# Pooled attention with an expert layer: the next pair's bounds ahead of the unit, and its K and V loads a step earlier

## The chip, the cores and the metric

The kernel runs on one core of one Trainium2 chip. The metric is the device time of the whole program in microseconds; the median of three runs before the change is 814.76 us (811.82 to 815.16). The profiled execution took 813.32 us.

## The reference

Attention over 4 batches and 8 heads with 64 columns; Q is averaged over pairs of neighbouring rows, so 576 rows of Q meet 1152 rows of K and V. Behind it, per row of 512 columns, a norm and two dense layers with a residual:

```
q_pool = q.reshape(B, H, S // 2, 2, D).mean(axis=3)
scores = q_pool @ k.transpose(0, 1, 3, 2) / sqrt(D)
attn   = softmax(scores) ; x = attn @ v            # then heads side by side: (4, 576, 512)
xn     = (x - mean) / sqrt(var + 1e-6) * g_ln
out    = x + maximum(xn @ w_ch1, 0) @ w_ch2
```

All is fp32. The kernel multiplies in fp16 with a high and a low half of each operand. So that the halves keep their precision it first looks for the largest absolute value of each Q, K and V (a bound), and scales by the power of two that this gives.

## The kernel before

**Tiling.** The heads go in pairs: 16 pairs, four to a batch (numbered from 0; p below). A pair has 576 x 2 rows of scores, worked in 9 steps of 128 rows, so there are 144 steps (i), and some 20 more in which only the dense layers run. The pair's first step is 9p; `i0 = (p - 1) * C` (L824) is the first step of the pair before it, and it is in those nine steps that pair p is prepared. The first batch (steps 0 to 35, `on_pe`) transposes its probabilities on TensorE. All later steps split them into a high and a low half and let a DMA transpose them (L440).

**One step** (`step`, L987) writes instructions in a fixed order, and each engine runs its own in that order. The minimum of the negated scores of step i on VectorE (`emit_max`, L410); the scores of step i + 1 on TensorE (`emit_s`, L390 and L398); then `flush`, which writes all that is kept in the list `evacs` (what empties the PSUM banks of the step before, on ScalarE and VectorE); the exponential and the high half on ScalarE (L417, L428); the low half of step i - 1 on VectorE, or on GpSimd in three of nine steps (L435 to L438), and the DMA transpose of that step on SP's queue; the output of step i - 4 on TensorE (`a_piece`, L480); one unit of the dense layers (`some_units`: 24 matmuls of L631, or 12 of L663); one preparation of pair p (`a_prep`); last what `todo` holds for the step, loads among it.

**PSUM.** Scores take two slots of three banks. In the third bank of a slot lie, side by side, the last 128 columns of the scores, the output (`ps` in L461) and the small results of the bounds (L193). The minimum of the next step reads that bank, so it waits for all that TensorE was told before to write there. ScalarE takes the scaled output from there (L540), and the scores two steps on wait for that. Units and preparations use banks 6 and 7 (`bank`, L552): if both are taken, `release` (L603) first writes what empties one.

**The bounds of pair p.** ScalarE takes the absolute maximum of each partition of K, Q and V (`bound`, L182) at steps i0 - 2 (Q), i0 + 1 (K) and i0 + 2 (V). At step i0 + 3 (step 3 of nine) `all_max` starts: TensorE transposes the maxima (L197), VectorE reduces them and sets up a diagonal (L200, L201). At step i0 + 4 TensorE spreads the result over all partitions (L208, "the spread"), and VectorE makes the scales of it (L231 to L234). K, Q and V are split with these.

**The preparations** (`PREPS`, L356) transpose K and Q on TensorE, one in each step from i0 + 4 on; ScalarE makes the high and VectorE the low half (L274, L271). GpSimd splits V in two halves (`take_v`, L239 and L266) at steps i0 + 5 and i0 + 7. K (`kr`) and V (`vr`) have one buffer each, so K of the next pair can't land before the last K preparation, nor V before V's second split. SP's queue carries the loads of K (two issues, L117 and L118), V (L121) and Q (L129), the stores (L684) and the transposes (L440), in the order in which they are written.

Of the kernel before, what the change touches and what calls it, by code (L numbers as in the profile page):

```python
# [24 lines left out]
def tile_pooled_attention_moe(  # L25
# [18 lines left out]
    nc = tc.nc  # L44
# [4 lines left out]
    C = S // 128  # L49
    HP = H // 2  # L50
# [109 lines left out]
    def pool_q(p, eng):  # L160
        x = raws[p, "q"]
        eng.tensor_tensor(x[:, :, 0], x[:, :, 0], x[:, :, 1], op=ALU.add)

    def dup_q(p, eng):
        x = raws[p, "q"]
        eng.tensor_copy(x[:, :, 1], x[:, :, 0])
# [171 lines left out]
    def prep_q_first():  # L338
# [17 lines left out]
    PREPS = (  # L356
        ((prep_k, 0), (prep_k, 2), (prep_q, 0), (prep_q, 1), (prep_k, 1), (prep_q, 2)),
        ((prep_k, 0), (prep_k, 2), (prep_q, 0), (prep_k, 1), (prep_q, 2), (prep_q, 1)),
    )


# [2 lines left out]
    def on_pe(i):  # L364

        return 0 <= i < HP * C
# [38 lines left out]
    def emit_max(i):  # L405

        st = steps[i]
        st["pe"] = p_p.tile([128, S], FP32, tag="pe", name="pe", bufs=3)
        nb = st["nb"] = sm_p.tile([128, 1], FP32, tag="nb", name="nb")
        nc.vector.tensor_tensor_reduce(  # L410
            out=st["pe"], in0=st["s"], in1=nought[:, 0:1].to_broadcast([128, S]),
            scale=pair[i // C]["sc"][:, 0:1], scalar=3.0e38, op0=ALU.add, op1=ALU.min, accum_out=nb,
        )

    def emit_exp(i):
        st = steps[i]
        nc.scalar.activation(out=st["pe"], in_=st["pe"], func=ACTF.Exp, scale=-1.0, bias=st["nb"])  # L417
# [32 lines left out]
    def emit_t_copy(i):  # L450
        st = steps[i]
        for a, b in ((0, 512), (512, S)):
            nc.scalar.copy(st["pt"][:, a:b], st["s"][:, a:b])  # L453
# [98 lines left out]
    def bank():  # L552
        for _ in range(2):
            for _ in free_banks:
                nbank[0] += 1
                n = nbank[1] = free_banks[nbank[0] % len(free_banks)]
                if n not in held and n not in waiting:
                    waiting.add(n)
                    return psum[:, n]
            n = nbank[0] + 1  # L560
            while free_banks[n % len(free_banks)] in held:
                n += 1
            release(free_banks[n % len(free_banks)])
# [34 lines left out]
    evacs, last = [], []  # L598

    def until(fns, n=None):  # L600
        evacs.extend((n, fn) for fn in fns)

    def release(n):  # L603
        waiting.discard(n)
        while any(m == n for m, _ in evacs):
            evacs.pop(0)[1]()

# [204 lines left out]
    def at(i, fn, *a):  # L812
        todo.setdefault(i, []).append((fn, a))
# [3 lines left out]
    def pre(i, fn, *a):  # L817
        early.setdefault(i, []).append((fn, a))
# [3 lines left out]

    for p in range(1, NP):
        i0 = (p - 1) * C  # L824
        at(max(i0 - 1, 0), load, p, "k", nc.sync)
        at(i0, load, p, "v", nc.sync)
        at(i0 + 1, bound, p, "k")
        if p == 1:
            pre(0, behind_scales)
            pre(i0 + 1, pool_q, p, nc.gpsimd)  # L830
            at(i0 + 1, dup_q, p, nc.gpsimd)
            at(i0 + 2, bound, p, "q")
        elif on_pe(i0):
            at(i0 - 4, load_q, p, (nc.sync,))
            at(i0 - 1, lambda p=p: calm.appendleft((lambda n: pool_q(p, nc.gpsimd), 0)))
            at(i0, lambda p=p: calm.appendleft((lambda n: dup_q(p, nc.gpsimd), 0)))
            at(i0 + 2, bound, p, "q")
        else:
            early_q = not on_pe(i0 - 6)
            at(i0 - (12 if early_q else 8), load_q, p, (nc.sync,))  # L840
            at(i0 - (6 if early_q else 4), pool_q, p, nc.vector)
            at(i0 - 2, bound, p, "q")
            at(i0 - 1, dup_q, p, nc.gpsimd)
        if not on_pe(p * C):
            at(i0 + 2, bound, p, "v")
        pre(i0 + 3, scales_reduce, p, 0, 2 if on_pe(p * C) else 3)
        for n in range(2):
            if on_pe(p * C):
                at(i0 + (5, 7)[n], gate)
            at(i0 + (5, 7)[n], take_v, p, n)  # L850
        for n, (fn, u) in enumerate(PREPS[p % HP // 2]):
            late = 1 if on_pe(i0) else 0
            pre(i0 + 4 + n + late, lambda fn=fn, p=p, u=u: preps.append((fn, p, u)))

# [24 lines left out]
    norms, fresh, turns = deque(), deque(), set()  # L879
# [79 lines left out]
    def a_prep():  # L959
        if preps:  # L960
            fn, p, u = preps.popleft()
            until(fn(p, u), nbank[1])
# [6 lines left out]
    def a_piece(i):  # L969
        pieces.extend(ready.pop(i, ()))  # L970
        for u in range(2 if len(pieces) > 2 and not on_pe(i) else 1):
            if pieces:
                n = pieces.popleft()
                pt = pts[n]
                ps = emit_pv(n, bank() if u or on_pe(n) else None)
                if on_pe(n):
                    ot = pt.rearrange("p a n -> p (a n)").bitcast(FP32)[0:65, 0:128]
                    until([lambda ot=ot, ps=ps: nc.scalar.activation(
                        out=ot, in_=ps[0:65, 0:128], func=ACTF.Identity, bias=eps
                    )], nbank[1])  # L980
                    turned.append((n, ot))
                    continue
                one, two = evac_pv(n, ps)
                until([one], nbank[1] if u else None)
                last.extend((two, lambda n=n: evacuated(n)))

    def step(i):  # L987
        live = i < NSTEP
        this[0] = i
        for fn, a in early.pop(i, ()):  # L990
            fn(*a)
        if live:
            emit_max(i)
        if on_pe(i - 1):
            emit_t_copy(i - 1)
            steps.pop(i - 1)
        while found:
            found.popleft()()
        first = on_pe(i - 1) or on_pe(i)
        final, last[:] = list(last), []  # L1000
        if first and not on_pe(i):
            a_piece(i)
        if on_pe(i):
            if i < 3:
                warm(16, bank())
            a_piece(i)
            a_prep()
            emit_exp(i)
        while scaled_out:
            scaled_out.popleft()()  # L1010
        if i + 1 < NSTEP:
            emit_s(i + 1)
            pv_slot[0] = i + 1
        else:
            free_banks[:] = [6, 7, 0, 1, 3, 4]
            pv_slot[0] += 1
        if on_pe(i):
            while fill:
                drip()
            flush()  # L1020
        else:
            flush()
            if live:
                emit_exp(i)
                emit_hi(i)
        for fn in final:
            fn()
        if 0 <= i - 1 < NSTEP and not on_pe(i - 1):
            emit_lo(i - 1)
            steps.pop(i - 1)  # L1030
            drip()
        norm(i)
        norms.extend(fresh)
        fresh.clear()
        red = None
        while soon or len(fill) > 3:
            drip()
        if on_pe(i):
            emit_t(i)
            if reds:  # L1040
                found.append(reds.popleft()())
        elif reds:
            red = reds.popleft()
            put = [None]

            behind = i % C == 3 or i % C == 4 and i not in turns
            if not behind:
                until([lambda: put[0]()])
        while turned:
            n, ot = turned.popleft()  # L1050
            emit_turn(n, ot, i)
        if not on_pe(i):
            if not first:
                a_piece(i)
            if red and not behind:
                put[0] = red()
            if i in turns:
                a_prep()
            some_units(i)
            if red and behind:  # L1060
                until([red()])
            if i not in turns:
                a_prep()
        for fn, a in todo.pop(i, ()):
            fn(*a)
        if calm and i < HP * C - 1:
            gate()
        for _ in range(1 if i < HP * C - 1 else 2):
            if calm:
                fn, n = calm.popleft()  # L1070
                fn(n)

    def warm(n, ps=None):
        ps = psum[:, 2, 0:128] if ps is None else ps[:, 0:128]
        for _ in range(n):
            nc.tensor.matmul(out=ps, lhsT=ident16, rhs=ident16, start=True, stop=True)

    with tc.manual_schedule():
# [67 lines left out]
        i = 0  # L1146
# [32 lines left out]
```

## Time and profile before

| | |
|---|---|
| median of three runs | 814.76 us |
| profiled execution | 813.32 us, span 811.5 us |
| TensorE busy | 781.8 us (96%) |
| VectorE, ScalarE, GpSimd busy | 598.6 (74%), 544.0 (67%), 342.5 us (42%) |
| granted TensorE clock | 1.00 of full speed in the whole span |
| DMA in 157 to 700 us / 700 to 811.5 us | busy share 0.86 / 0.06 |

The first batch ends near 157 us; from there to some 700 us attention and the dense layers share the steps (4.4 to 5.5 us each); behind that only dense layers are left. In the rows further down PE is TensorE, PEld its weight loads, DVE VectorE, ACT ScalarE, POOL GpSimd and SPq the DMA queue of SyncE. What stands in brackets behind an instruction is how long its engine stood idle before it, and which engine's instruction ended that.

### The profile page before, as it was taken

Reading aid. Unit: us, or ns where it says so; the run is one execution under the profiler, and the core shown is the slowest. Engines: PE = TensorE matmul, PEld = TensorE weight load, DVE = VectorE, ACT = ScalarE, POOL = GpSimd, SP = SyncE. Lnnn points to the kernel's source line nnn. Section 1 sums busy time; section 2 is a strip of 40 time slices with the busy share of each in tenths; the row PEclk is TensorE's granted clock in tenths of the full one; section 3 lists DMA queues with packets and bytes.
Section 4 is the critical chain, followed back from the end, with each engine's and each line's share of the span. In section 5 each row is a group of like instructions: output and inputs, shape, how many; then the busy total and the mean of one; then the engine's idle time right before and its main releaser. Section 6 shows DMA issues by size and latency. Waiting matters only on the chain.

```text
span 811.5 us, 21278 instructions
## 1 busy us (share of the span) xinstructions
PE 781.8 (96%) x8936; PEld 551.8 (68%) x8936; DVE 598.6 (74%) x1179; ACT 544.0 (67%) x789; POOL 342.5 (42%) x342
## 2 busy tenths in 40 slices
PE   8999999989989999989999999999999999999997
PEld 6788887767565656567666665767575757766764
DVE  5899999878898986898687877887786867521221
ACT  5889888777767777787677686877677776211010
POOL 2012333576999862665453535537161532300000
PEclk9999999999999999999999999999999999999999
DMA  9736545025998989896989798987979786401001
GB/s 282 241 107 219 192 135 172 2 72 109 168 181 154 179 167 201 164 213 116 202 143 220 147 212 145 186 163 144 197 135 196 131 145 121 86 1 27 14 1 27
DMA packets 276017, 115.95 MB, mean 143 GB/s; under 512 B 259280, under 2 KB 259280, under 8 KB 275920
## 3 DMA queue, kind: packets, MB, share of 16 engines
q1 hardware_dynamic: 275440, 113.63, 67.9%
q8 instruction: 70, 1.15, 0.6%
q10 hardware_dynamic: 480, 0.95, 0.4%
q14 instruction: 27, 0.22, 0.1%
HBM read 46.14 MB, written 4.72 MB: 63 GB/s over the span
## 4 chain that ended last, share of the span: by engine, by line
PE 63%; DVE 16%; ACT 7%; DMA 6%; issue 4%; SPq 2%; POOL 2%; ACTq 0%; DVEq 0%
PE psum L663 19%; PE psum L631 17%; PE psum L390 7%; PE psum L480 6%; PE psum L471 5%; DVE pe L410 5%; PE psum L447 3%; DVE hl L437 3%; DMA vr<-in_v_dram 2%; PE psum L398 2%; ACT pe L417 2%; SPq L440 2%; DMA kr<-in_k_dram 1%; DMA stage<-in_moe_w_ch_dram 1%; PE psum L321 1%
## 5 line engine op out<-in xcount | busy, mean ns | idle before, releaser
L410 DVE CUSTOM_DVE_ANT_0 pe<-psum,nought,sc 128x1152 f32<-128x1152 f32 x144 | 203.0, 1410 | 25.2 <-PE psum L197 9.7
L417 ACT ACTIVATE pe<-pe,nb 128x1152 f32<-128x1152 f32 x144 | 180.4, 1253 | 32.4 <-DVE nb L410 31.2
L663 PE MATMUL psum<-wsl,ht 128*128 128x512 f16 x864 | 196.6, 379 | 2.5 <-DVE ht L645 2.1
L631 PEld LDWEIGHTS <-wsl 128*128 128x128 f16 x1920 | 169.6, 98 | 25.3 <-issue 7.6
L631 PE MATMUL psum<-xn,wsl 128*128 128x256 f16 x1536 | 176.3, 273 | 6.6 <-DVE xb L677 3.8
L663 PEld LDWEIGHTS <-ht 128*128 128x128 f16 x864 | 81.1, 98 | 90.9 <-issue 3.1
L428 ACT ACTIVATE hl<-pe 128x1152 f16<-128x1152 f32 x108 | 125.6, 1163 | 3.4
L390 PE MATMUL psum<-kt,qt 64*128 64x512 f16 (+1 forms) x960 | 120.2, 380 | 1.0 <-ACT qt L274 0.7
L644 ACT ACTIVATE ht<-psum 128x512 f16<-128x512 f32 x72 | 42.7, 593 | 115.4 <-PE psum L631 112.2
L437 DVE SCALAR_TENSOR_TENSOR hl<-pe,hl 128x1152 f16<-128x1152 f32 x72 | 113.3, 1573 | 0.0
L480 PE MATMUL psum<-vt,pt 128*128 128x65 f16 (+2 forms) x3240 | 106.8, 193 | 0.0
L645 DVE SCALAR_TENSOR_TENSOR ht<-psum,ht 128x512 f16<-128x512 f32 x72 | 49.3, 685 | 72.3 <-ACT ht L644 72.3
L480 PEld LDWEIGHTS <-pt 128*128 128x128 f16 (+1 forms) x3240 | 98.4, 100 | 2.6 <-issue 0.2
L239 POOL TENSOR_SCALAR pe<-pe 128x1152 f32<-128x1152 f32 x36 | 41.4, 1149 | 118.8 <-ACT hl L428 118.8
L435 POOL TENSOR_TENSOR hl<-pe,hl 128x1152 f16<-128x1152 f32 x36 | 85.6, 2378 | 3.0
L471 PE MATMUL psum<-pt,vt 128*65 128x128 f32 (+1 forms) x720 | 77.4, 263 | 1.3 <-DVE kt L271 1.3
L471 PEld LDWEIGHTS psum<-pt,vt 128*65 128x65 f32 x720 | 71.5, 138 | 1.5 <-DVE kt L271 1.5
L390 PEld LDWEIGHTS <-qt 64*128 64x128 f16 (+1 forms) x960 | 31.7, 96 | 47.6 <-issue 29.5
L398 PEld LDWEIGHTS <-qt 128*128 128x128 f16 (+1 forms) x320 | 17.6, 99 | 65.8 <-issue 65.6
L677 DVE SCALAR_TENSOR_TENSOR xb<-psum,inv,xb 128x512 f32<-128x512 f32 x32 | 23.8, 744 | 36.3 <-PE psum L663 36.1
L271 DVE SCALAR_TENSOR_TENSOR qt<-psum,s,qt 128x512 f16<-128x512 f32 (+2 forms) x49 | 29.7, 606 | 28.3 <-ACT qt L274 27.9
L453 ACT COPY pt<-psum 128x512 f32<-128x512 f32 x72 | 44.2, 639 | 7.1 <-PE psum L447 6.0
(116 smaller groups left out, 939.9 us busy)
## 6 DMA issues: line engine op xcount, KB each, us to landing
stage<-in_moe_w_ch_dram SPq DMA_DIRECT2D x32, 512.0 KB, 6.2
kr<-in_k_dram SPq DMA_DIRECT2D x16, 576.0 KB, 4.7
vr<-in_v_dram SPq DMA_DIRECT2D x16, 576.0 KB, 5.0
qr<-in_q_dram SPq DMA_DIRECT2D x31, 288.0 KB, 4.8
out_dram<-xb SPq DMA_DIRECT2D x28, 128.0 KB, 3.0
pt<-hl SPq DMA_TRANSPOSE x108, 4.9
kr<-in_k_dram SPq DMA_DIRECT2D x16, 64.0 KB, 4.5
out_dram<-xb ACTq DMA_DIRECT2D x4, 128.0 KB, 2.6
```

The lines of the kernel that those rows point to most:

```text
L390: nc.tensor.matmul(out=sp[o:o + w, c0:c0 + 512], lhsT=qt[r:r + 64, qa, q0:q0 + w], rhs=kt[r:r + 64, ka, h], start=(a == 0), stop=(a == 2),)
L410: nc.vector.tensor_tensor_reduce(out=st["pe"], in0=st["s"], in1=nought[:, 0:1].to_broadcast([128, S]), scale=pair[i // C]["sc"][:, 0:1], s ...
L417: nc.scalar.activation(out=st["pe"], in_=st["pe"], func=ACTF.Exp, scale=-1.0, bias=st["nb"])
L428: nc.scalar.activation(out=hl[:, 0], in_=st["pe"], func=ACTF.Copy, scale=2.0 ** 15)
L435: nc.gpsimd.tensor_tensor(hl[:, 1], st["pe"], hl[:, 0], op=ALU.subtract)
L437: nc.vector.scalar_tensor_tensor(hl[:, 1], st["pe"], 2.0 ** 15, hl[:, 0], op0=ALU.mult, op1=ALU.subtract)
L453: nc.scalar.copy(st["pt"][:, a:b], st["s"][:, a:b])
L471: nc.tensor.matmul(out=ps[0:65, q0:q0 + w], lhsT=vt[:, h, c], rhs=pt[:, 128 * u + q0:128 * u + q0 + w], start=(u == 0), stop=(u == C - 1),)
L480: nc.tensor.matmul(out=dst[:, 0:n], lhsT=pt[:, a + u, q0:q0 + w], rhs=vt[:, h, c, x0:x0 + n], start=(u == 0 and a == 0 and n == 65), stop= ...
L631: nc.tensor.matmul(out=ps[:, o:o + n], lhsT=wsl[:, 8 * w + cc, wa, f * 128:f * 128 + 128], rhs=xn[:, xa * KD + cc, 0:n], start=(m == 0), s ...
L645: lambda: nc.vector.scalar_tensor_tensor(lo, pv, 0.0, hi, op0=ALU.max, op1=ALU.subtract),
L663: nc.tensor.matmul(out=ps, lhsT=hv[0][:, ha, f, t * 128:t * 128 + 128], rhs=wsl[:, 8 * w + 4 + f // 2, wa, (f % 2) * DM:(f % 2) * DM + DM] ...
```

## The change

Five edits. The spread (step 4 of nine) is always written in front of the unit; before, it was behind it unless a transpose of the norm (`turns`) fell into that step. The transpose of the maxima (step 3) stays behind the unit. What VectorE does for the bounds is put at the head of `evacs` with the mark -1, so it comes first in the next `flush`, and `release` writes it before anything else. K of pairs 6 to 15 is loaded one step sooner, and V of pairs 10 to 15 too. In pairs 10 to 15 the first split of V comes a step later, where it stands behind GpSimd's low half. Pairs 5, 8, 9, 12 and 13 get a third list of preparations, with the second half of K one place earlier and the second part of Q one later.

```diff
@@ PREPS
+        ((prep_k, 0), (prep_k, 2), (prep_q, 0), (prep_k, 1), (prep_q, 1), (prep_q, 2)),
@@ release(n)
         waiting.discard(n)
+        while evacs and evacs[0][0] == -1:
+            evacs.pop(0)[1]()
         while any(m == n for m, _ in evacs):
             evacs.pop(0)[1]()
@@ for p in range(1, NP)
-        at(max(i0 - 1, 0), load, p, "k", nc.sync)
-        at(i0, load, p, "v", nc.sync)
+        at(max(i0 - (2 if i0 > HP * C else 1), 0), load, p, "k", nc.sync)
+        at(i0 - (1 if i0 > 2 * HP * C else 0), load, p, "v", nc.sync)
...
-            at(i0 + (5, 7)[n], take_v, p, n)
-        for n, (fn, u) in enumerate(PREPS[p % HP // 2]):
+            at(i0 + (6 if i0 > 2 * HP * C else 5, 7)[n], take_v, p, n)
+        for n, (fn, u) in enumerate(PREPS[p % HP // 2 or (0 if on_pe(i0) else 2)]):
@@ step(i)
-            put = [None]
-            behind = i % C == 3 or i % C == 4 and i not in turns
-            if not behind:
-                until([lambda: put[0]()])
+            behind = i % C == 3
+            def reduce():
+                evacs.insert(0, (-1, red()))
...
             if red and not behind:
-                put[0] = red()
+                reduce()
             if i in turns:
                 a_prep()
             some_units(i)
             if red and behind:
-                until([red()])
+                reduce()
```

## Rows read from the trace of the kernel before

**Rows 1.** the page: busy time, share and instructions of each engine

```profile
PE 781.8 (96%) x8936; PEld 551.8 (68%) x8936; DVE 598.6 (74%) x1179; ACT 544.0 (67%) x789; POOL 342.5 (42%) x342
```

**Rows 2.** TensorE's waits, 157 to 700 us: total us, times, longest

```profile
PE psum L398 <- ACT xb L540: 4.8, 6, 1.6
PE psum L631 <- DVE xb L677: 3.8, 4, 1.6
PE psum L631 <- DVE ht L645: 2.8, 7, 0.8
PE psum L208 <- DVE diag L201: 2.2, 2, 1.1
PE psum L663 <- DVE ht L645: 2.1, 5, 0.5
...
PE psum L663 <- DVE xb L677: 0.4, 1, 0.4
PE psum L321 <- DVE ht L645: 0.4, 1, 0.4
```

**Rows 3.** timeline, two steps ahead of pair seven's spread: start, duration, instruction

```profile
269.96 2.78 PE L631 MATMUL psum<-xn,wsl 128*128 128x256 f16 x24 [1.42 <-DVE xb L677]
```

**Rows 4.** ScalarE's waits for K and V in front of their bounds

```profile
ACT kt L182 <- DMA vr<-in_v_dram: 10.4, 8, 2.6
...
ACT kt L182 <- DMA kr<-in_k_dram: 8.2, 4, 3.4
```

**Rows 5.** timeline of pair ten, steps 3 to 6 of nine

```profile
405.15 0.75 DVE L162 TENSOR_TENSOR qr<-qr 128x576 f32<-128x576 f32 x1
...
405.76 0.27 PE L197 MATMUL psum<-ident,acc 128*3 128x128 f32 x1
...
406.07 1.42 DVE L410 CUSTOM_DVE_ANT_0 pe<-psum,nought,sc 128x1152 f32<-128x1152 f32 x1 [0.17 <-PE psum L197]
...
407.10 0.27 PE L398 MATMUL psum<-kt,qt 128*128 128x128 f16 x2 [0.32 <-ACT xb L540]
...
407.21 0.98 PE L480 MATMUL psum<-vt,pt 128*128 128x65 f16 x27
...
408.03 2.78 PE L631 MATMUL psum<-xn,wsl 128*128 128x256 f16 x24
408.33 0.27 DVE L200 TENSOR_REDUCE mx<-psum 3x1 f32<-3x129 f32 x1
408.63 0.21 DVE L201 SCALAR_TENSOR_TENSOR diag<-psum,mx,ident 3x3 bf16<-3x3 f32 x1
...
410.99 1.42 DVE L410 CUSTOM_DVE_ANT_0 pe<-psum,nought,sc 128x1152 f32<-128x1152 f32 x1 [0.89 <-PE psum L208]
...
413.39 2.78 PE L631 MATMUL psum<-xn,wsl 128*128 128x256 f16 x24 [0.29 <-DVE ht L645]
...
418.64 2.53 PE L663 MATMUL psum<-wsl,ht 128*128 128x512 f16 x11 [0.46 <-DVE ht L645]
```

**Rows 6.** timeline of pair seven, the same place

```profile
276.23 2.08 DVE L162 TENSOR_TENSOR qr<-qr 128x576 f32<-128x576 f32 x1
...
278.24 1.41 DVE L410 CUSTOM_DVE_ANT_0 pe<-psum,nought,sc 128x1152 f32<-128x1152 f32 x1
...
278.30 0.98 PE L480 MATMUL psum<-vt,pt 128*128 128x65 f16 x27
```

**Rows 7.** timelines of pair six and pair eight: SP's queue and one output

```profile
217.27 2.81 SPq L440 DMA_TRANSPOSE pt<-hl  x1
...
224.61 0.98 PE L480 MATMUL psum<-vt,pt 128*128 128x65 f16 x27
...
305.21 0.52 SPq L117 DMA_DIRECT2D kr<-in_k_dram  x1
...
306.38 5.48 SPq L440 DMA_TRANSPOSE pt<-hl  x1
```

**Rows 8.** the page, DMA issues: KB each, median us to landing

```profile
pt<-hl SPq DMA_TRANSPOSE x108, 4.9
```

## The prediction

> **What bounds the kernel now.** I read the engines' busy times first: TensorE works in 96% of the span, the others in 74% or less [rows 1]. So a microsecond counts where TensorE stands still, and the second view is what it waits for between 157 and 700 us, where attention of batches two to four runs beside the expert layers [rows 2]; the 112 us behind that are matmuls alone and move with the end of attention as a block. Three kinds of wait in that list lie around the bounds of the next pair:
>
> A. A unit (24 or 12 matmuls of the expert layers) or a preparation waits for VectorE to empty the bank that it is to write: 2.8, 2.1, 0.4, 0.4 and part of the 3.8 us. Of these 3.8, two waits of 1.6 and 1.4 stand two steps ahead of the spread [rows 2, 3], where GpSimd still splits weights; the change doesn't touch them. That leaves 6.5 us in 16 waits.
> B. The last score matmuls wait for ScalarE to take the output out of that bank: 4.8 us in six [rows 2]. ScalarE works in order, and it stood 8.2 us for K and 10.4 us for V in front of their bounds [rows 4].
> C. Twice the spread matmul, where it stands in front of the unit, waits 1.1 us for VectorE [rows 2].
>
> The third view is a timeline of one pair, the tenth [rows 5]. The reader is to see an order there. The transpose of the bounds runs behind the unit at 405.76. The minimum over the next scores shares its bank, so it starts only at 406.07. VectorE then empties the output and the unit, and only then reduces the bounds (408.33 and 408.63, 0.27 and 0.21 us). The spread follows the next unit, and the next minimum stood 0.89 us for it. From there VectorE is late for two steps: the next unit waits 0.29 us, the one behind it 0.46.
>
> **The change part by part.** Eleven pairs (five to fifteen) have their bounds outside the first batch.
>
> *Spread in front of the unit (D).* This is added wait. Behind the spread on TensorE's queue stand the unit and the first preparation of K, so all later steps wait with it. VectorE's minimum takes 1.42 us, then come 0.27 and 0.21 and some 0.05 for handing over [rows 5], so the spread can start 1.95 us behind the minimum's start. In pair ten that is 406.07 + 1.95 = 408.02. The output matmuls end at 407.21 + 0.98 = 408.19, but 0.32 of that is a wait of kind B in front of them, so 407.87 without it: a wait of 0.15. A unit that follows without a wait starts inside the end of the output matmuls (408.03 against 408.19 [rows 5]), and any wait loses that overlap: 0.16 more. So 0.31 a pair. Where VectorE is late it is more: in pair seven the pooling of Q took 2.08 us against 0.75 in pair ten, and the minimum began at 278.24. So the spread can go at 280.19, and the output matmuls end at 278.30 + 0.98 = 279.28: 0.91, with the overlap 1.07 [rows 5, 6]. Pair six looks like seven. In pair five a transpose stands behind that of the bounds, and the spread needn't wait. Sum: 8 x 0.31 + 2 x 1.07 = 4.6 us lost. Bounds: nothing, and 11 x 1.07 = 11.8.
>
> *VectorE's part first, and what the earlier spread gives.* The reductions move ahead of what empties output and unit, which is 0.5 us later by that. The unit of this step takes the other bank, so nobody waits for it, except in pair five, where the unit of the step already waits 0.3 and now waits 0.7, and the next 0.5 for 0.3. VectorE loses its 0.89 [rows 5], and the scales stand first in the next step, so ScalarE makes the high half of K about 1.5 us sooner and VectorE no longer idles for it. I work out pair ten: VectorE starts the next minimum at 410.1 (410.99 less 0.89). Minimum 1.4, scales 0.3, output 0.4 and unit 0.7 end 2.8 later, at 412.9. TensorE comes to that bank at 413.1 (413.39 less 0.29; the 0.31 of D and the 0.32 of B cancel): the wait of 0.29 goes, and that of 0.46 a step later with it. So goes A: 6.5 us and 16 x 0.16 for the overlap, 9.1 us, of which 1.4 in four waits stay (pair five 1.2, pairs six and seven 0.1 each, since the scales now come ahead of the unit there), with their overlap 2.0. Gain 7.1. Bounds: nothing (VectorE as late as now) and 9.1.
>
> *The two spreads that already stood in front* (C): their 2.2 us go, and what is left is counted in D. Gain 2.2.
>
> *K a step sooner, V in six pairs (ten to fifteen).* K's two issues and V's one stand on SP's queue between the transposes of the probabilities, and are moved past one of those each. K was issued at 305.21 in pair eight [rows 7], behind a transpose that it now overtakes, so 3 to 5 us sooner, as long as ScalarE's longest wait for it. It needs the single buffer: the second half of the old K has to be through TensorE, and that is why the third list of preparations puts it one place ahead of the second half of Q. That swap costs nothing: the Q half is read three steps behind its old place and two behind the new, and both preparations take one slot. What stays of B I put at 1.0: pair nine's wait, which follows a step that had no unit, so that TensorE is ahead there, and a rest in pair six, whose V keeps its place. Gain 3.8. Bounds: nothing and 4.8.
>
> *What K delays.* A transpose takes 2.8 us of the queue alone, and 5.48 behind K [rows 7], that is until K has landed. Now the transpose one step earlier gets those 2.7 us, while the next two come sooner. In pair six it was issued at 217.27, lands 4.9 later [rows 8] at 222.2, and its output matmuls start at 224.61 [rows 7]: 2.4 to spare, so 0.3 to 0.4 us lost there. The other pairs I take to have more room. Bounds: nothing, and 0.8 in each of ten pairs. The Trainium skill ("DMA: Bandwidth & Descriptors", section "Two DMAs through the same engine are not ordered") says that descriptors of one queue start in order but are pipelined. By it the transpose would lose only K's two issues of 0.5 us, and the sum would be 8.5 for 8.1; the 5.48 us disagree with it.
>
> *V's first split a step later, behind GpSimd's low half.* Nothing: the split is read seven steps on, and the same three instructions run in the other order. The low half comes sooner by that. If the cover goes, V's load waits for the split in its single buffer and holds SP's queue, which costs what a late transpose costs. *Emptying the bounds first when a bank is wanted*: only order, nothing.
>
> **Sum.** 7.1 + 2.2 + 3.8 - 4.6 - 0.4 = 8.1 us. From the profiled execution's own 813.32 us (span 811.5 and 1.8 around it) that makes 805.2. The median of the runs shown, 814.76, is 1.44 above that execution, so I forecast 806.7.
>
> **The rivals.**
> 1. *VectorE is the bound at the spread* (the other side). If the minimum starts 0.9 us late in all eleven pairs, as in pair seven, TensorE stands 11 x 1.07 = 11.8 us in front of units that today run meanwhile, and VectorE comes out no sooner, so A stays whole. 3.8 + 2.2 - 11.8 = 5.8 us slower: 820.6. It decides from a wait of 0.55 us a pair. For it: VectorE's pooling of Q stands right ahead of the minimum, and GpSimd's work lengthens it to 2.08 us. Against it: pair ten's 0.75. The Trainium skill ("SBUF — State Buffer", section "Who interferes with whom") says that a VectorE instruction with two operands from that memory contends with GpSimd's reads; the 2.08 us agree, and a GpSimd that gets its scales sooner could carry this into other pairs.
> 2. *The transposes come late.* If K and V in front of other transposes cost 0.8 us in each of ten pairs, the 8.1 are gone: 814.8. For it: the 5.48 us. Against: the copies leave the places where they delay transposes now.
> 3. *The waits move on.* Half of A and of B returns in the next steps, since VectorE and ScalarE have as much to do as before: 3.5 + 1.9 + 2.2 - 4.6 - 0.4 = 2.6 faster, 812.2. For it: three waits in a row in one pair. Against: most steps between the pairs have no wait at all.
> 4. *The loads are sooner and nobody notices* (the change doesn't do that part): B stays, 4.3 faster, 810.5.
>
> **How the numbers follow.** A measurement of this kernel tells 0.5% from no change, 4.1 us: below 810.7 is faster, above 818.8 slower. Forecast 0.60 (803 to 809), the fourth rival 0.10, the third 0.14, the second 0.10, the first 0.06. Faster: 0.60, half of the fourth and a third of the third: 0.70. Slower 0.06, the same 0.24. The range: if all of A, B and C went and the spread cost only its 2.5, 13.6 us, the time would be 801; I leave the last of that out and begin at 802.5. Above it takes in the third rival and half of the second: 814.5.
>
> **What would show it.** In the changed kernel the spread runs ahead of the unit in all pairs, with waits of some 0.15 us and two near 0.9. TensorE's waits for the emptying of units fall from 16 to four or so. The score matmuls wait for ScalarE once or twice. ScalarE's waits for K and V in front of their bounds nearly go. The minimum's waits for the spread go. I am wrong if the spread's waits come to more than 8 us, if output matmuls begin to wait for transposes, or if waits of VectorE's banks turn up in steps that had none.

## The result: 806.43 us, where 806.7 was forecast

The changed kernel takes 806.43 us (median of 4 runs, 806.34 to 807.48) against 814.33 us before: a ratio of 0.9911, 95% interval 0.9887 to 0.9935. A second set of runs gave 806.48 against 815.0, ratio 0.9888 (0.9874 to 0.9903). The profiled execution took 807.48 us with a span of 805.7.

TensorE is busy for 97% of the shorter span, the others as before [rows 1]:

```profile
PE 784.3 (97%) x8936; PEld 553.5 (69%) x8936; DVE 594.3 (74%) x1179; ACT 544.3 (68%) x789; POOL 340.7 (42%) x342
```

The first 36 steps and all behind step 143 are the same program in both kernels. So I measure the stretch between: from the first score matmul of step 36 to that of step 143, in the profiled execution. It was 511.21 us before and is 502.98 now, 8.23 less; the rest behind it took 130.13 and 130.15. A second profile of the changed kernel (E9 below) has 503.26, so two profiles of one program can differ by some 0.3 us in it. The span alone would mislead here, since the opening of this execution ran at a lower clock and lost 2.36 us (last section).

In what follows each fence has the line numbers of its own kernel; in the changed one the score matmuls are L391 and L399, the minimum L411, the output L481, the units L634 and L666, and what empties them L648 and L680.

TensorE's waits between 157 and 700 us (total us, times, longest), to be read against [rows 2]:

```profile
PE psum L208 <- DVE diag L201: 2.6, 8, 0.9
PE psum L634 <- DVE xb L680: 1.7, 2, 0.9
...
PE psum L634 <- DVE ht L648: 1.2, 3, 0.5
PE psum L399 <- ACT xb L541: 1.2, 2, 0.7
...
PE psum L587 <- DVE qt L271: 0.5, 1, 0.5
PE psum L481 <- DMA pt<-hl: 0.4, 1, 0.4
```

What the reader is to see: of 12 waits of units for `ht` three are left, all those in front of L666 are gone, the waits of scores for ScalarE went from six to two, and in their place stand eight waits at the spread, 2.6 us in all, of which the longest is 0.9. One wait of an output for a transpose is new, 0.4 us.

The timeline of pair ten (start, duration, instruction), the same place as [rows 5]:

```profile
404.40 0.27 PE L197 MATMUL psum<-ident,acc 128*3 128x128 f32 x1
...
404.71 1.42 DVE L411 CUSTOM_DVE_ANT_0 pe<-psum,nought,sc 128x1152 f32<-128x1152 f32 x1 [2.35 <-PE psum L197]
...
405.48 0.98 PE L481 MATMUL psum<-vt,pt 128*128 128x65 f16 x27
...
406.05 0.28 DVE L200 TENSOR_REDUCE mx<-psum 3x1 f32<-3x129 f32 x1
...
406.36 0.21 DVE L201 SCALAR_TENSOR_TENSOR diag<-psum,mx,ident 3x3 bf16<-3x3 f32 x1
...
406.62 0.16 PE L208 MATMUL psum<-diag,ones 128*128 128x3 bf16 x1 [0.17 <-DVE diag L201]
...
406.65 2.78 PE L634 MATMUL psum<-xn,wsl 128*128 128x256 f16 x24
...
408.66 1.41 DVE L411 CUSTOM_DVE_ANT_0 pe<-psum,nought,sc 128x1152 f32<-128x1152 f32 x1
...
410.00 0.16 DVE L231 TENSOR_SCALAR s<-psum 128x3 int32<-128x3 int32 x1
...
410.67 0.98 PE L481 MATMUL psum<-vt,pt 128*128 128x65 f16 x27
...
411.49 2.78 PE L634 MATMUL psum<-xn,wsl 128*128 128x256 f16 x24
...
416.12 2.10 PE L666 MATMUL psum<-wsl,ht 128*128 128x512 f16 x9
```

The reductions now follow the minimum at once (406.05, 406.36). The spread starts 1.91 us behind the minimum's start and has waited 0.17; the unit behind it has lost its overlap with the output's end. The next minimum (408.66) no longer stands for the spread, and the scales are the first thing behind it. The two units that follow start at 411.49 and 416.12 without a wait, inside the end of the output matmuls.

Pair seven, where VectorE is late [rows 6]:

```profile
277.92 1.97 DVE L162 TENSOR_TENSOR qr<-qr 128x576 f32<-128x576 f32 x1
...
279.81 1.40 DVE L411 CUSTOM_DVE_ANT_0 pe<-psum,nought,sc 128x1152 f32<-128x1152 f32 x1
...
281.72 0.17 PE L208 MATMUL psum<-diag,ones 128*128 128x3 bf16 x1 [0.77 <-DVE diag L201]
...
286.90 2.78 PE L634 MATMUL psum<-xn,wsl 128*128 128x256 f16 x24
```

The pooling of Q is as long as it was (1.97 us), the minimum begins late, and the spread waits 0.77 us for it.

ScalarE's waits in front of the bounds, against [rows 4]:

```profile
ACT kt L182 <- DMA vr<-in_v_dram: 8.0, 4, 2.3
...
ACT kt L274 <- DVE e L232: 6.9, 9, 1.9
```

K's waits are gone. V's are left in the four pairs whose V kept its place. The high half of K waits 6.9 us for the scales; in the kernel before it was 21.9:

```profile
ACT kt L274 <- DVE e L232: 21.9, 10, 3.0
```

### The profile page after: what moved, and what is told of

It reads as the page before. It is cut to its first block, busy times and chain, and to the rows that moved or that the text cites. A ratio compares the mean times of both kernels' runs of the same rounds, so it can differ in the third digit from the quotient of the medians.

```text
span 805.7 us, 21290 instructions
## 1 busy us (share of the span) xinstructions
PE 784.3 (97%) x8936; PEld 553.5 (69%) x8936; DVE 594.3 (74%) x1179; ACT 544.3 (68%) x789; POOL 340.7 (42%) x342
## 4 chain that ended last, share of the span: by engine, by line
PE 76%; DVE 12%; ACT 5%; issue 3%; POOL 2%; DMA 1%; SPq 0%; ACTq 0%; POOLq 0%; DVEq 0%
PE psum L666 21%; PE psum L634 20%; PE psum L391 9%; PE psum L481 8%; PE psum L472 5%; DVE pe L411 4%; PE psum L448 3%; PE psum L399 3%; DVE hl L438 2%; PE psum L321 1%; ACT pe L418 1%; DMA vr<-in_v_dram 1%; PE psum L285 1%; PE psum L1081 1%; PE psum L587 1%
## 5 line engine op out<-in xcount | busy, mean ns | idle before, releaser
L411 DVE CUSTOM_DVE_ANT_0 pe<-psum,nought,sc 128x1152 f32<-128x1152 f32 x144 | 203.1, 1410 | 27.1 <-PE psum L197 13.9
L666 PE MATMUL psum<-wsl,ht 128*128 128x512 f16 x864 | 196.6, 379 | 0.0
L634 PEld LDWEIGHTS <-wsl 128*128 128x128 f16 x1920 | 169.2, 98 | 24.5 <-issue 6.9
L634 PE MATMUL psum<-xn,wsl 128*128 128x256 f16 x1536 | 176.3, 272 | 3.1 <-DVE xb L680 1.7
L666 PEld LDWEIGHTS <-ht 128*128 128x128 f16 x864 | 80.8, 98 | 88.5 <-issue 0.8
L391 PE MATMUL psum<-kt,qt 64*128 64x512 f16 (+1 forms) x960 | 120.4, 382 | 0.9 <-ACT qt L274 0.7
L438 DVE SCALAR_TENSOR_TENSOR hl<-pe,hl 128x1152 f16<-128x1152 f32 x72 | 110.5, 1535 | 0.0
L481 PE MATMUL psum<-vt,pt 128*128 128x65 f16 (+2 forms) x3240 | 106.8, 193 | 0.4 <-DMA pt<-hl 0.4
L481 PEld LDWEIGHTS <-pt 128*128 128x128 f16 (+1 forms) x3240 | 98.3, 100 | 3.4 <-DMA pt<-hl 0.6
L648 DVE SCALAR_TENSOR_TENSOR ht<-psum,ht 128x512 f16<-128x512 f32 x72 | 49.4, 686 | 65.5 <-ACT ht L647 65.4
L391 PEld LDWEIGHTS <-qt 64*128 64x128 f16 (+1 forms) x960 | 31.7, 96 | 47.5 <-issue 29.3
L399 PEld LDWEIGHTS <-qt 128*128 128x128 f16 (+1 forms) x320 | 17.4, 99 | 62.9 <-issue 62.5
L680 DVE SCALAR_TENSOR_TENSOR xb<-psum,inv,xb 128x512 f32<-128x512 f32 x32 | 23.8, 745 | 36.6 <-PE psum L666 36.5
```

What stands on the lines that cost most here:

```text
L391: nc.tensor.matmul(out=sp[o:o + w, c0:c0 + 512], lhsT=qt[r:r + 64, qa, q0:q0 + w], rhs=kt[r:r + 64, ka, h], start=(a == 0), stop=(a == 2),)
L411: nc.vector.tensor_tensor_reduce(out=st["pe"], in0=st["s"], in1=nought[:, 0:1].to_broadcast([128, S]), scale=pair[i // C]["sc"][:, 0:1], s ...
L438: nc.vector.scalar_tensor_tensor(hl[:, 1], st["pe"], 2.0 ** 15, hl[:, 0], op0=ALU.mult, op1=ALU.subtract)
L481: nc.tensor.matmul(out=dst[:, 0:n], lhsT=pt[:, a + u, q0:q0 + w], rhs=vt[:, h, c, x0:x0 + n], start=(u == 0 and a == 0 and n == 65), stop= ...
L634: nc.tensor.matmul(out=ps[:, o:o + n], lhsT=wsl[:, 8 * w + cc, wa, f * 128:f * 128 + 128], rhs=xn[:, xa * KD + cc, 0:n], start=(m == 0), s ...
L648: lambda: nc.vector.scalar_tensor_tensor(lo, pv, 0.0, hi, op0=ALU.max, op1=ALU.subtract),
```

## The experiments

All but E10 were timed beside the kernel before. "Stretch" is steps 36 to 143 in each profile. E2 is an edit of the kernel before, E3 one of E2's kernel; the others are edits of the changed kernel. K's loads, V's loads and the third list of preparations were not tried one by one, so what each of them gives is not shown.

| kernel | median us | ratio to before (95%) | stretch us |
|---|---|---|---|
| before | 814.33 | | 511.21 |
| changed | 806.43 | 0.9911 (0.9887 to 0.9935) | 502.98 |
| E1 order of the bounds alone | 808.16 | 0.9931 (0.9914 to 0.9947) | 504.75 |
| E2 loads alone | 811.19 | 0.9962 (0.9949 to 0.9976) | 507.83 |
| E3 spread in front, VectorE's part not first | 814.19 | 0.9986 (0.9970 to 1.0002) | 512.08 |
| E4 VectorE's part first, spread behind | 809.04 | 0.9926 (0.9909 to 0.9944) | 505.33 |
| E5 V's split at its old step | 807.68 | 0.9904 (0.9889 to 0.9919) | 504.51 |
| E6 changed, transpose in front, seven pairs | 804.34 | 0.9880 (0.9859 to 0.9900) | 502.84 |
| E7 the same, six pairs | 803.66 | 0.9856 (0.9840 to 0.9873) | 500.58 |
| E8 the same in all pairs, V sooner from pair six on | 800.59 | 0.9820 (0.9804 to 0.9837) | 497.36 |

**E1, the order of the bounds alone.** The edit keeps `release`, `behind` and `reduce` of the change and undoes the rest:

```diff
-        at(max(i0 - (2 if i0 > HP * C else 1), 0), load, p, "k", nc.sync)
-        at(i0 - (1 if i0 > 2 * HP * C else 0), load, p, "v", nc.sync)
+        at(max(i0 - 1, 0), load, p, "k", nc.sync)
+        at(i0, load, p, "v", nc.sync)
...
-            at(i0 + (6 if i0 > 2 * HP * C else 5, 7)[n], take_v, p, n)
+            at(i0 + (5, 7)[n], take_v, p, n)
-        for n, (fn, u) in enumerate(PREPS[p % HP // 2 or (0 if on_pe(i0) else 2)]):
+        for n, (fn, u) in enumerate(PREPS[p % HP // 2]):
```

> The kernel before with the order of the bounds alone: spread always in front of the unit, VectorE's part first; loads, preparations and splits of V as before. My theory (two independent parts): TensorE's waits for the emptying of units behind the bounds fall from 16 to about four and the two 1.1 us waits at the spread go, while eleven short waits at the spread come in: 7.1 + 2.2 - 4.6 = 4.7 us faster than before, near 809.6. The six waits of the scores for ScalarE (4.8 us) stay. Rival 'the loads do it all': within 1 us of before. Rival 'the order does it all': near 806.5.

Measured: 808.16, 5.9 us less than the 814.02 of before in the same set, and 6.46 in the stretch. TensorE's waits in its stretch of 157 to 700 us:

```profile
PE psum L398 <- ACT xb L540: 3.9, 6, 1.3
...
PE psum L208 <- DVE diag L201: 1.9, 7, 0.8
PE psum L633 <- DVE ht L647: 1.5, 4, 0.5
```

The waits behind the bounds go as forecast, and those for ScalarE stay in number (six, 3.9 us for 4.8). The part is 1 to 2 us larger than my 4.7: the spread waits 1.9 us where I had 3.0, and two of the scores' waits shrink though no load was moved (the step in pair eight that waited 0.82 us is 0.89 shorter, that in pair fourteen that waited 1.65 is 1.03 shorter).

**E2, the loads alone.** The lines marked - in the diff of E1, with the third list of preparations, are put into the kernel before, and nothing else of the change.

> The kernel before with the loads alone: K (and V from pair ten on) a step sooner, V's first split later, the third list of preparations; the order of the bounds as before. My theory: the waits of the scores for ScalarE go except about 1 us, 0.4 us is lost where a transpose of pair six comes late: 3.4 us faster than before, near 810.9; the 16 waits behind the bounds and the two of 1.1 us at the spread stay. Rival 'nobody notices sooner loads': within 1 us of before.

Measured: 811.19, 2.8 us less, and 3.38 in the stretch. The same view:

```profile
PE psum L632 <- DVE ht L646: 2.8, 7, 0.8
...
PE psum L664 <- DVE ht L646: 2.0, 5, 0.5
PE psum L399 <- ACT xb L541: 1.7, 4, 0.7
PE psum L208 <- DVE diag L201: 1.6, 2, 1.1
```

The 12 waits for `ht` and the two at the spread stand, the latter at 1.6 us for 2.2; the scores' waits fall to 1.7 us. Outputs wait for transposes here, 1.5 us in three. In pair six that costs nothing (its step takes 6.17 us for 6.16), but in pair eight, where nothing else waits in that step, a wait of 0.27 makes it 4.86 us for 4.41. The two parts add up to 9.84 us in the stretch and together give 8.23, so 1.6 us of waiting was there for either to take: the two steps named under E1 are shorter in both.

**E3, the spread in front with VectorE's part in its old place** (E2's kernel, whose loads stay, with this edit):

```diff
-            behind = i % C == 3 or i % C == 4 and i not in turns
+            behind = i % C == 3
...
             if red and behind:
                 until([red()])
```

> The changed kernel with one part undone: the spread stays in front of the unit in all pairs, but VectorE reduces the bounds only behind the emptying of output and unit, as before. My theory: the spread then waits about 1.1 us (0.4 for the output, 0.7 for the unit) longer in nine pairs and 0.4 longer in the last two, so some 9 to 10 us of waits at the spread more than in the changed kernel; one or two of them are given back where a unit behind waited, so 813 to 816, the same as before: putting the spread in front pays only with VectorE's part first. Rival 'the place of the spread is what counts': within 1.5 us of the changed kernel, near 807.

Measured: 814.19, and 512.08 us in the stretch, 9.1 more than the changed kernel. The same view:

```profile
PE psum L208 <- DVE diag L201: 10.8, 11, 1.8
```

Eleven waits at the spread, 10.8 us: in the median all that the change gains is gone. Beside E2, which has the same loads, the median is 3.0 us more. The stretch is 4.25 us longer than E2's, but this profile is of the slowest of twelve runs, and by estimate 1.7 us of the 4.25 went to a lower clock (a granted clock of 0.83 over the 10 us from 236 to 246). Five of the runs took 810.9 to 812.3 us and seven 814.0 to 815.5; what parts the two groups is not shown. All are over 4 us slower than the changed kernel's second set.

**E4, the other half: VectorE's part first, the spread behind the unit.**

```diff
-            behind = i % C == 3
+            behind = i % C == 3 or i % C == 4 and i not in turns
```

> The changed kernel with the spread behind the unit again (except in the two pairs where it stood in front before), VectorE's part still first. My theory (each half needs the other): the waits at the spread fall from 2.6 us to about 0.3, with their lost overlap some 4 us less; but the minimum stands for the spread again (0.9 to 1.1 us in pairs eight, ten to fifteen) and VectorE is late for the units of the next two steps, so 10 or more waits of 0.3 to 0.5 us come back, some 5 to 7 us with the overlap. Steps 36 to 143 take 504 to 506 us, 1 to 3 us slower than the changed kernel. Rival 'VectorE's part first does all': 499 us, faster than the changed kernel by 4.

Measured: 809.04 and 505.33 us in the stretch, 2.35 more than the changed kernel. First the waits of TensorE, then those of VectorE:

```profile
PE psum L634 <- DVE ht L648: 4.8, 7, 1.0
```

```profile
DVE pe L411 <- PE psum L208: 3.8, 6, 1.0
```

The minimum stands for the spread again in six pairs, and units wait seven times, 4.8 us, for three times and 1.2 us in the changed kernel. The loads and the reductions first give 2.5 us over E2 (507.83 to 505.33), and the spread in front another 2.35 on top of that. In front it pays only with VectorE's part first.

**E5, V's first split back at its old step.**

```diff
-            at(i0 + (6 if i0 > 2 * HP * C else 5, 7)[n], take_v, p, n)
+            at(i0 + (5, 7)[n], take_v, p, n)
```

> The changed kernel with V's first split back at its old step, in front of GpSimd's low half. My theory: nothing that TensorE sees, within 1.5 us of the changed kernel, since the split is read seven steps on; GpSimd's low half and the transpose behind it come about 3 us later, and output matmuls still don't wait. Rival 'the split holds up the queue': V's load or transposes of steps 5 and 6 come late, output matmuls wait or ScalarE waits for V, 2 us or more slower.

Measured: 807.68, 1.2 us more than the changed kernel in the same set (four runs each), 1.53 in the stretch, of which 1.23 lie in one step of pair fourteen (5.60 us for 4.37). I had costed this edit at nothing, and that is wrong by this much. The timeline of pair fourteen, SP's queue and TensorE:

```profile
561.03 0.52 SPq L117 DMA_DIRECT2D kr<-in_k_dram  x1
...
562.18 3.69 SPq L441 DMA_TRANSPOSE pt<-hl  x1
...
569.62 0.99 PE L481 MATMUL psum<-vt,pt 128*128 128x65 f16 x27 [1.05 <-DMA pt<-hl]
```

An output waits 1.05 us for its transpose, which the changed kernel doesn't have there: K is issued at 561.03 for 558.95, though the steps around it begin 0.96 us earlier in this profile, and the transposes behind it follow. GpSimd's low half comes behind the split (it ends at 551.06 for 549.03) and holds up SP's queue.

**E6 and E7, the transpose of the bounds in front of the unit as well.** In the changed kernel VectorE's minimum still stands 13.9 us for that transpose. It needs ScalarE's bound of V, which from pair ten on is done 2 us before the output matmuls end. E6 had a bound one pair too low, and pair nine was in it; E7 has it right:

```diff
-            behind = i % C == 3
+            behind = i % C == 3 and i < 2 * HP * C          # E6
+            behind = i % C == 3 and i < 2 * HP * C + C      # E7
```

> The changed kernel with the transpose of the bounds in front of the unit too, in pairs ten to fifteen, whose V is bounded about 2 us before the output matmuls of that step end. My theory: the minimum of the next step, which shares the bank, starts some 2.6 us sooner, VectorE has the reductions done before the spread's turn, and the six waits of 0.17 us at the spread with their lost overlap of 0.16 go: 1.8 us faster than the changed kernel, near 804.6. Rival 'TensorE then waits for ScalarE's bound of V': a wait of up to 1 us in front of each of the six transposes, 806 to 812.

Measured for E6: 804.34, but the stretch is only 0.14 us shorter than in the changed kernel. TensorE's timeline in pair nine, and the busy time of that window (PE busy, PEld, DVE, ACT, POOL, granted clock, DMA):

```profile
353.72 0.30 PE L399 MATMUL psum<-kt,qt 128*64 128x128 f16 x4 [0.72 <-ACT xb L541]
...
356.60 0.27 PE L197 MATMUL psum<-ident,acc 128*3 128x128 f32 x1 [1.65 <-ACT kt L182]
356.71 4.45 PE L634 MATMUL psum<-xn,wsl 128*128 128x256 f16 x24
```

```profile
356.00:361.00 5.00, 4.40 (x25) 3.21 (x25) 3.80 (x7) 3.06 (x5) 3.20 (x5) 0.66 1.18 197
```

Both of my theories were at work: six pairs lost their wait at the spread, and in the seventh TensorE waited 1.65 us for ScalarE's bound of V, after 0.72 in the same step. Then the granted clock fell to 0.66, and the unit took 4.45 us for 2.78.

> The transpose of the bounds in front of the unit in pairs ten to fifteen alone; the run before had pair nine in it by mistake, whose V was late: 1.65 us of waiting and 1.7 us more for the next unit at a granted clock of 0.66. My theory (that one pair ate the gain of the other six): pair nine's step is 3.5 us shorter and its next 1.2 us longer than there, so 2.3 us faster than that run, near 802, and steps 36 to 143 take some 500.5 us against 502.98 in the changed kernel. Rival 'the transpose in front brings nothing': steps 36 to 143 stay at 502 to 503.

Measured for E7: 803.66, and 500.58 us in the stretch, as expected. The median is 0.7 us lower than E6's, not 2.3. In the two profiles the opening hides the rest: up to step 36 it took 171.70 us in E7 and 170.29 in E6 (last section). For the other runs the opening is not on record.

**E8, in all eleven pairs, with V a step sooner from pair six on:**

```diff
-        at(i0 - (1 if i0 > 2 * HP * C else 0), load, p, "v", nc.sync)
+        at(i0 - (1 if i0 > HP * C else 0), load, p, "v", nc.sync)
...
-            behind = i % C == 3
+            behind = False
```

> The same in all eleven pairs, with V's load a step sooner from pair six on, so that pairs six to nine have their V bounded in time. My theory: the two waits of 0.8 us at the spread in pairs six and seven shrink to about 0.2 or less and pair nine's go, some 2 to 3 us faster than with six pairs: near 799.5. Rival 'V in front of one more transpose': output matmuls of pairs six to nine wait for late transposes (two of them had 0.05 us to spare), 1 to 3 us lost; rival 'bounds still late': a wait of over 1 us at a transpose and a granted clock under 1 behind it, 803 or more.

Measured: 800.59 us, 1.8% under before and 5.8 us under the changed kernel: the best version of this study. TensorE's waits, the same stretch:

```profile
PE psum L634 <- DVE xb L680: 1.4, 2, 1.1
...
PE psum L481 <- DMA pt<-hl: 1.3, 2, 1.0
```

The waits at the spread are gone from the list. Outputs wait 1.3 us for transposes in pairs six and seven, which is the rival's mechanism. In pair six it costs nothing, since the unit of that step has to wait for VectorE anyway: the step takes 5.97 us here and 5.98 in the changed kernel, with 0.97 and 0.40 us of waiting for the transpose. In pair seven the step is 0.63 us longer (6.20 for 5.57); its output waits 0.32, but the unit behind it then waits 1.14 for VectorE, whose minimum starts 1.04 us behind the scores for 0.42, so the late transpose is not what ends last there.

**E9, the changed kernel once more** (no edit).

> The changed kernel once more. In its profile the granted clock was 0.61 between 12 and 20 us and the first 36 steps took 2.36 us longer than in the profile of before, whose instructions there are the same. My theory: that is chance of the single execution and not of the change, so among these runs some have a granted clock of 1.000 and about 2.3 us less, near 804, others near 806.4. Rival 'the changed program always opens at the lower clock': all runs at 806.3 or more.

Measured: 806.48 us; three runs at a clock of 0.996 or 0.997 took 806.25 to 806.81, one at 1.000 took 805.03. So it is chance, though for this kernel a frequent one. In this profile the opening took 171.51 us, 1.31 more than in that of before and 1.05 less than in the first of the changed kernel: there are more than two cases (last section).

**E10, K on ScalarE's DMA queue** (one run, not in the table).

```diff
-        at(max(i0 - (2 if i0 > HP * C else 1), 0), load, p, "k", nc.sync)
+        at(max(i0 - (2 if i0 > HP * C else 1), 0), load, p, "k", nc.scalar if i0 > HP * C else nc.sync)
```

> The changed kernel with K of pairs six to fifteen issued on ScalarE's DMA queue instead of SP's, at the same step. Question: does a transpose that follows K take 5.5 us instead of 2.8 because it stands behind K on one queue, or because K is in flight at all? If the queue: transposes beside K take 2.7 to 2.8 us of SP. If the flight: they still take 4 to 5.5 us. The time of the kernel is not the point; ScalarE has two issues and a wait for TensorE more in each pair, so some 2 to 8 us slower than the changed kernel.

Measured: 831.79 us. The longest transpose, in pair nine:

```profile
348.12 0.38 ACTq L117 DMA_DIRECT2D kr<-in_k_dram  x1
...
353.05 10.99 SPq L441 DMA_TRANSPOSE pt<-hl  x1
```

A transpose that starts 5 us behind K, on another queue, takes 10.99 us; that K landed 13.8 us after its issue. In six pairs, where K was nearly there, transposes took 2.5 to 3.4. In the other four, where K was still in flight, they took 5.59 to 10.99. So in this run it is the copy in flight and not its place in the queue that goes with a slow transpose, and on SP's queue it was at most 5.56 us before (pair thirteen; 5.48 in [rows 7]). Why the two slow each other so much in two pairs stays open. The 25 us are not the transposes' alone: TensorE waited 9.3 us for two of them, and ScalarE stood 2.6 to 3.3 us at its issues of K in each of the ten pairs, 29.5 us in all.

## Why the prediction was right, and where it was right by luck

*A, units that wait for their bank*: 2.0 us with the lost overlap were to stay, in pairs five to seven. What stayed: 0.43 and 0.54 in pair five (0.7 and 0.5 forecast), 0.14 each in pairs six and seven (0.1; too short for the list above, which begins at 0.15), and 0.25 in pair thirteen, which I had not seen. The mechanism and the size hold.

*B, scores that wait for ScalarE*: 1.0 was to stay, 1.2 did, both in pair nine: the step behind the one without a unit (0.73), and one more of 0.43 in the next.

*C and D, the spread*: 1.95 us from the minimum to the spread were worked out, 1.91 came. Waits of 0.15 in most pairs and 0.91 in two were forecast; 0.17 in six pairs, 0.85 and 0.77 in pairs six and seven were measured, 2.6 us in all for 3.0. E3 and E4 show that the spread in front is worth something only because the reductions come first.

The gain of C was mis-sized. In pairs nine and thirteen, where the spread already stood in front, the terms make 0.8 us each (1.1 less 0.31), and the pairs gave 0.25 and 0.06. Pair thirteen, first the kernel before, then the changed one:

```profile
539.03 0.16 PE L208 MATMUL psum<-diag,ones 128*128 128x3 bf16 x1 [1.08 <-DVE diag L201]
...
539.53 2.84 PE L631 MATMUL psum<-xh,wsl 128*128 128x128 f16 x48
```

```profile
535.16 0.17 PE L208 MATMUL psum<-diag,ones 128*128 128x3 bf16 x1 [0.17 <-DVE diag L201]
...
536.07 2.84 PE L634 MATMUL psum<-xh,wsl 128*128 128x128 f16 x48 [0.25 <-DVE ht L648]
539.06 0.63 PE L587 MATMUL psum<-ident,xs 128*128 128x128 f32 x4 [0.15 <-DVE kt L271]
```

The wait at the spread is 0.91 shorter, but the two instructions behind it now wait for VectorE, and the step is only 0.16 us shorter (6.49 for 6.65). In pair nine the scores wait 0.43 for ScalarE and a transpose 0.21 for VectorE in its place. This is the third rival, in two pairs.

*The late transpose* in pair six was forecast as a wait of 0.3 to 0.4 us, and it is there:

```profile
218.87 0.58 SPq L117 DMA_DIRECT2D kr<-in_k_dram  x1
...
220.08 4.02 SPq L441 DMA_TRANSPOSE pt<-hl  x1
...
227.56 0.99 PE L481 MATMUL psum<-vt,pt 128*128 128x65 f16 x27 [0.40 <-DMA pt<-hl]
...
229.39 2.78 PE L634 MATMUL psum<-xn,wsl 128*128 128x256 f16 x24 [0.84 <-DVE xb L680]
```

The transpose behind K takes 4.02 us, its output waits 0.40. But it isn't a loss as I had it: the unit behind it waited 1.60 us for VectorE before and now waits 0.84, and the step is 0.18 us shorter than it was (5.98 for 6.16). I had put the two waits of 1.6 and 1.4 [rows 2, 3] down as untouched; they fell to 1.7 together. That step failed, on the good side, by 0.6 us of step time in the two pairs. It is the order of the bounds that shortens them: the two steps take 5.96 and 5.54 us in E1, without the loads, and 6.17 and 5.99 in E2, as before (6.16 and 5.99).

*V's later split*, costed at nothing, is worth 1.2 us (E5).

The sum was 8.1 us in the profiled execution's own time, and the stretch gave 8.23. It is as near as that because errors cancel. In seven of the eleven pairs (five, eight, ten to twelve, fourteen, fifteen) the terms come within 0.2 us of what the pair's steps gave. Pairs six and seven gave 1.1 us more than their terms, pairs nine and thirteen 1.2 less; that these two are of one size is luck. By parts errors cancel too: the bounds alone gave 6.46 in the stretch (E1) where the terms make 4.7, the loads alone 3.38 (E2) where they make 3.8 - 0.4 = 3.4, and 1.6 of it is counted in both.

Of the rivals, waits that move on are in pairs nine and thirteen and in those 1.6 us, far from half of A and B; VectorE as the bound at the spread is what pairs six and seven are, and what E3 is in all pairs; the one late transpose in the changed kernel's profile stands where something else waits anyway, though with the same loads a late transpose cost up to 0.6 us in pair eight of other runs (4.86 us in E2 and 5.00 in E4 for a step of 4.41); sooner loads that nobody notices are refuted by E2.

## What to carry to other kernels

When a small chain (here: transpose, reduce, spread) hops between a busy engine and a slack one, first put its part at the head of the slack engine's queue, then move the busy engine's part forward; in the other order the busy engine pays for the slack one's queue (E3 against E4). An instruction that shares a PSUM bank with the next step's input delays that step from where it stands in the queue, so its place is worth more than its 0.27 us. And a new wait counts only if nothing behind it would have waited: compare the length of the step, not the list of waits.

## What the runs showed of the hardware that was not expected

**The granted clock fell behind short waits in a dense stretch (E6, E3).** In E6 TensorE had 0.72 and 1.65 us without work within 4 us and the next 5 us ran at 0.66 of full speed, part of it at 1.2 GHz; the unit there took 1.67 us longer. That step took 8.94 us, against 5.45 in E7, and the one behind it 5.34 against 6.51, so the wait of 1.65 us cost 2.3 in all. In E3 a single wait of 1.75 us, at the spread of pair six, went with a granted clock of 0.83 between 236 and 246 us. But no fall followed a wait of 2.36 us in pair seven of E3, nor one of 1.65 in pair fourteen of the kernel before. What decides it stays open.

**The opening runs at the lower clock in some executions and not in others.** The instructions of the first 36 steps are the same in all twelve profiles. Granted clock by window in the changed kernel's (the number before the DMA share):

```profile
12.00:20.00 8.00, 6.41 (x43) 4.53 (x42) 4.48 (x8) 4.39 (x7) 3.46 (x5) 0.61 1.04 289
```

In four profiles (before, E2, E6, E8) it is 1.00 there, and the first score matmul of step 36 comes at 170.1 to 170.3 us; in five (E1, E3, E5, E7, E9) it is 0.79, and that matmul comes at 171.3 to 171.7; in three (the changed kernel's first, E4, E10) it is 0.61 or 0.62, and it comes at 172.6 to 172.7. TensorE waits 1.47 us for VectorE near 14 us in the profile of before and in that of the changed kernel alike, so that wait alone doesn't decide it. Up to 2.6 us of a difference between two executions can be the opening alone, and a comparison of profiles has to leave it out.

**A DMA transpose and a copy in flight hold each other up**, on one queue (4.0 us for 2.8 behind K) and across two (up to 10.99 in E10, where that K landed 13.8 us after its issue and six others in 5.4 to 6.7). The Trainium skill ("DMA: Bandwidth & Descriptors", section "Issuing engines are not separate DMA queues") says that DMAs of several engines run on the same 16 engines and interleave, so that another engine saves issue time alone; E10 agrees that another queue brings no relief, and shows a price that the sentence doesn't have.
